# A sequential attention and feed-forward step at batch one: fewer TensorE instructions in the tail, one early touch of its program instead of two, a straight program on the sync engine

## The chip, the cores and the metric

The kernel runs on one core of one Trainium2 chip. The core has five engines with their own instruction streams: TensorE (PE, matrix products), VectorE (DVE), ScalarE (ACT), GpSimd (POOL) and SyncE (SP, here the issuer of nearly all transfers), and sixteen DMA engines that move data between HBM and the on-chip memory SBUF. Results of TensorE go to a second memory, PSUM, in eight banks. Engines wait for each other through semaphores. The metric is the device time of one execution in microseconds; smaller is better.

## What is computed

One token passes a grouped-query attention block with a cache of 65,536 positions and then a gated feed-forward block without a nonlinearity; both have a layer normalisation ahead of them and a residual addition behind.

```python
B, Sq, D = 1, 1, 512
Hq, Hkv, Sk, Dh = 32, 8, 65536, 128

def _A_ref(x, k_cache, v_cache, wq, wo):
    q = (x @ wq).reshape(B, Sq, Hq, Dh).transpose(0, 2, 1, 3)
    k = jnp.repeat(k_cache, rep, axis=1)
    v = jnp.repeat(v_cache, rep, axis=1)
    scores = jnp.einsum("bhqd,bhkd->bhqk", q, k) * (Dh ** -0.5)
    p = _softmax(scores, axis=-1)
    o = jnp.einsum("bhqk,bhkd->bhqd", p, v)
    return o.transpose(0, 2, 1, 3).reshape(B, Sq, Hq * Dh) @ wo

def _B_ref(x, w_gate, w_up, w_down):          # F = 1792
    return ((x @ w_gate) * (x @ w_up)) @ w_down

h  = x + _A_ref(_layernorm(x), k_cache, v_cache, wq, wo)
h2 = h + _B_ref(_layernorm(h), w_gate, w_up, w_down)
```

All of it is in 32-bit floats. The K and V caches alone are 537 MB, and every byte of them is read once.

## The kernel before

**Data.** The host lays K and V out as 64 chunks of 128 partitions by 16,384 floats (8.39 MB): for each of the 8 KV heads four chunks of K and then four of V. Two SBUF buffers, `kv[0]` and `kv[1]`, take the even and the odd chunks. Weights come through `wqo_sb` (the query weights of the next head beside the output weights of the present one), and at the end, when the caches are through, through the same two buffers: the gate and up weights `wg_t`, `wu_t` lie in `kv[0]`, the down weights `wd_t` in `kv[1]`, as 14 column blocks of 512 floats (numbered 0 to 13; `NC` is 14).

**The sync engine (lines 118 to 158, 479).** It issues the transfers in order. After the query weights of head 0 it jumps to a block of its program that lies far behind (`sp_far`, the lines ahead of `pe_main`) and back to `sp_main`; then come the first two chunks, and from there one chunk for each buffer that VectorE reports as free (semaphore `free`). An odd chunk raises four semaphores `s_vp`, one by the transfer and three by the sync engine's own increments, because the very last V chunk comes in four pieces (`V_CUTS`) that TensorE takes one at a time. At the end it issues the gate weights in one transfer, the up weights in three (`U_CUTS`), the down weights in six (`D_CUTS`: blocks 0-3, 4-7, 8-9, 10-11, 12, 13), and jumps to `fin`, where it waits for the result and stores four rows of `y`.

**TensorE (from `pe_main`).** It starts with two far jumps, to `pe_early` (within the first K chunk's code) and `pe_late` (between the gate and the up projection), each with one semaphore increment, and comes back to `pe_main`. In each head (`head()`): the query row for the head's four query heads (L371), turned into columns of `sm[0]` by products with a one (L375); four K chunks and four V chunks, each 32 products of 32 stationary columns (`st`) with 512 columns of the chunk (`chunk()`, L365), where four neighbouring products use four column groups of the array. Ahead of the V chunks come the softmax's maximum and the transposes of the exponentials (L380 to L387). Behind the last V chunk: the four groups of `orow` are added over partitions (L396), the softmax sums spread over all partitions (L400), and the heads' output multiplied with the output weights (L404). A product of 32-bit floats is executed as two matmul instructions, each with its own weight load; a transpose is one.

**VectorE (`dve_main` to `dve_tail`).** It sets up the constants and the first normalisation, evacuates PSUM, takes maxima, and scales. Behind the last V chunk of a head it frees the buffer, adds `orow` (L277), takes the reciprocal of the sums (L283), writes `o_pad` (L284), and adds the attention output to `acc`, the running residual (L287), where the row sum `rsum` comes along.

**The tail.** Once through the heads, the residual row `acc` must become columns. TensorE multiplies slices of `acc` with a selector (L413) and subtracts the mean in the same PSUM group (L415, `nmean`); VectorE copies it into `hn_pad` (L307). Then: the gate projection (L426, `wg_t`), the variance (L437), the up projection (L426 again, `wu_t`), the product of both with the normalisation's scale in two halves (`f_sb`, L320), its columns (L441 to L448, `f_pad`), and the down projection. Blocks below `SIDE` (8) go as one 512-wide product each, with four column groups, into `ps[1]` (L458), and VectorE adds `acc` to the four groups to give `res` (L328). The other blocks, 8 to 13, go as four 128-wide products each into `pva` (L473), and the groups of `res` are summed into the same place by products with a selector (L467). VectorE copies `pva` to `y` (L330), and the sync engine stores it (L479).

**Order.** Every engine works its own list in order. `take(e, s, n)` waits until a semaphore holds n and takes n off; `turn()` lets TensorE wait for the next step of VectorE's counter `dt` in the tail; `mine()` is VectorE's wait for its own last result.

Of the kernel before, what the change touches and what calls it, by code (L numbers as in the profile page):

```python
# [8 lines left out]
P = 128  # L9
# [34 lines left out]
def body(nc, xr, kvd, wq0, wqo, wo7, wg, wu, wd, out):  # L44
    pe_e, dve_e, act_e, pool_e, sp = nc.tensor, nc.vector, nc.scalar, nc.gpsimd, nc.sync

    def tile(name, *shape, align=32):
        return nc.alloc_sbuf_tensor(name, list(shape), F32, align_bytes=align).ap()
# [17 lines left out]
    wq_sb, wo_sb = wqo_sb[:, 0], wqo_sb[:, 1]  # L66
    xn, ln_q2 = tile("xn", P, KT), tile("ln_q2", P, KT)
    ln_s, ln_m, ln_v, ln_t, ln_r = (tile(n, 1, 1) for n in ("ln_s", "ln_m", "ln_v", "ln_t", "ln_r"))
# [40 lines left out]
    def take(e, s, n=1):  # L109
        e.wait_ge(s, n).then_inc(s, -n)  # L110
# [15 lines left out]
    sp.dma_start(wq_sb, wq0).then_inc(s_wq, 16)  # L126
    sp.br("sp_far")
    nc.switch_bb("sp_main", parent=None)
    even(0)
# [25 lines left out]
    for p, (lo, hi) in enumerate(zip(D_CUTS, D_CUTS[1:])):  # L155
        cs = slice(lo * D, hi * D)
        sp.dma_start(wd_t[:, cs], wd[:, cs]).then_inc(s_wd[p], 16)
    sp.br("fin")
    for e in (pool_e, act_e, dve_e, pe_e):
        e.br("others")  # L160
    nc.switch_bb("others", parent=None)
    dve_e.br("dve_far")
    pe_e.br("pe_early")

    take(act_e, da)
    act_e.activation(ln_t, ln_v, AF.Sqrt, bias=eps_t[0:1, 0:1], scale=1.0 / D).then_inc(ad, 1)
    pool.tick(pool_e.memset(ident, 0.0))
    pool_e.wait_ge(pool.sem, pool.n)
    c_ident = pool.tick(pool_e.affine_select(
        out=ident, in_=ident, compare_op=ALU.not_equal, fill=1.0, base=0,  # L170
        pattern=[[-1, P]], channel_multiplier=1))
    c_zero = pool.tick(pool_e.memset(qx, 0.0))
    for t in (o_pad, hn_pad, f_pad, sel_pad, acc):
        c_pads = pool.tick(pool_e.memset(t, 0.0))

    pool_e.br("fin")

    act_e.br("dve_main")
# [38 lines left out]
    with nc.Fori(0, HKV, engines=DVE_ACT):  # L217
# [41 lines left out]
        for n in range(NT):  # L259
            if n == 2:  # L260
                dve_e.sem_inc(tok, 2)
                take(dve_e, pd, 2)
                dve_e.sem_inc(da, 1)
            take(dve_e, pd)
            dve_e.tensor_copy(  # L265
                st[:, :, 0:16].rearrange("p g (b h) -> p b g h", h=REP),
                ptp[n % 2].rearrange("p (b g h) -> p b g h", b=4, h=REP)).then_inc(qt, 1)
            if n == NT - 1:
                mine(dve_e.tensor_reduce(out=l1, in_=sums, axis=AX.X, op=ALU.add))
                mine(dve_e.tensor_scalar(  # L270
                    out=l4, in0=sel_h, scalar1=l1[:, 0:1], scalar2=None, op0=ALU.mult))
# [11 lines left out]
        mine(dve_e.reciprocal(linv, sm[1][:, 0:REP]))  # L283
        dve_e.tensor_tensor(  # L284
            out=o_pad[:, :, 0], in0=sm[0][:, 0:REP], in1=linv, op=ALU.mult).then_inc(tok, 1)
        take(dve_e, pd)
        mine(dve_e.scalar_tensor_tensor(  # L287
            out=acc, in0=attn, scalar=1.0, in1=acc, op0=ALU.mult, op1=ALU.add,
            accum_out=rsum[:, 0:1]))

    take(act_e, pa)
# [3 lines left out]
    def mine(inst):  # L295
        inst.then_inc(own, 1)
        take(dve_e, own)
    dve_e.br("dve_tail")
    with nc.body("dve_far", parent=None, valid_engines=DVE_ONLY):
        dve_e.sem_inc(spare, 1)  # L300
        dve_e.br("dve_main")
    nc.switch_bb("dve_tail")
    dve_e.sem_inc(dt, 1)
# [4 lines left out]
    dve_e.sem_inc(dt, 1)  # L308
    mine(dve_e.tensor_tensor(out=ln_q2, in0=hn_pad[:, :, 0], in1=hn_pad[:, :, 0], op=ALU.mult))
# [17 lines left out]
    take(dve_e, pd)  # L327
    dve_e.tensor_tensor(out=res, in0=ps[1], in1=acc, op=ALU.add).then_inc(dt, 1)  # L328
    take(dve_e, pd)
    c_y = dve.tick(dve_e.tensor_copy(y, pva[:, 0:P]))  # L330
    dve_e.br("fin")

    with nc.body("sp_far", parent=None, valid_engines=SP_ONLY):
        sp.sem_inc(spare, 1)
        sp.br("sp_main")
    mm = pe_e.matmul
# [15 lines left out]
    def chunk(buf):  # L352
        pieces = [(0, 32, s_kv)] if not buf else [
            (lo, hi, p) for lo, hi, p in zip(V_CUTS, V_CUTS[1:], s_vp)]
        for lo, hi, p in pieces:
            take(pe_e, p, 16)
            for w in range(lo, hi):
                r, j = divmod(w, 4)
                if (buf, w) == (0, 29):
                    pe_e.br("pe_rest")  # L360
                    with nc.body("pe_early", parent=None, valid_engines=PE_ONLY):
                        pe_e.sem_inc(spare, 1)
                        pe_e.br("pe_late")
                    nc.switch_bb("pe_rest")
                i = mm(ps[buf][32 * j:32 * j + 32, :], st[:, 8 * j + r, :],  # L365
                       kv[buf][:, w * 512:(w + 1) * 512], start=(r == 0), stop=(r == 7))
        i.then_inc(kd, 1)

    def head():
        for k in range(KT):  # L370
            i = mm(ptp[0][0:1, :], xn[:, k:k + 1], wq_sb[:, k, :], start=(k == 0), stop=(k == KT - 1))  # L371
        i.then_inc(pd, 1)
        take(pe_e, tok)
        for r in range(REP):
            i = mm(sm[0][:, r:r + 1], qrow[0:1, r * P:(r + 1) * P], ones[0:1, 0:1], start=True, stop=True)  # L375
        i.then_inc(pd, 1)
        with nc.Fori(0, 4, engines=PE_ONLY) as u:
# [15 lines left out]
            chunk(1)  # L393
        take(pe_e, tok)
        for b in range(4):
            i = mm(sm[0][:, 0:REP], orow[:, b * P:(b + 1) * P], sel_b[:, 4 * b:4 * b + 4],  # L396
                   start=(b == 0), stop=(b == 3))
        i.then_inc(pd, 1)
        take(pe_e, tok)
        mm(sm[1][:, 0:REP], ones, l4, start=True, stop=True).then_inc(pd, 1)  # L400
        take(pe_e, s_w, 16)
# [6 lines left out]
    with nc.Fori(0, HKV, engines=PE_ONLY):  # L408
        head()

    turn()
    for k in range(KT):
        mm(sm[1][:, k:k + 1], acc[:, k * P:(k + 1) * P], sel_1, start=(k == 0), stop=False)  # L413
    turn()
    mm(sm[1][:, 0:KT], nmean, ones[:, 0:KT], start=False, stop=True).then_inc(pd, 1)  # L415
    turn()

    def project(acc, w, sems, c):
# [9 lines left out]
        i.then_inc(c, 1)  # L428

    project(ptp[0], wg_t, [s_wg], pa)  # L430
    pe_e.br("pe_up")
    with nc.body("pe_late", parent=None, valid_engines=PE_ONLY):
        pe_e.sem_inc(spare, 1)
        pe_e.br("pe_main")
    nc.switch_bb("pe_up")
    turn()
# [13 lines left out]
    i2.then_inc(pd, 1)  # L450
    turn()
    for c in range(SIDE):
        if c == 8:
# [6 lines left out]
    i.then_inc(pd, 1)  # L460
    if SIDE <= 8:
        turn()
    for c in range(SIDE, NC):
        if c == 12:
            turn()
            for j in range(4):
                mm(pva[32 * j:32 * j + 32, 0:P], sel_pad, res[:, j * P:(j + 1) * P],  # L467
                   start=False, stop=False)
        if c in D_CUTS:
            pe_e.wait_ge(s_wd[D_CUTS.index(c)], 16)  # L470
        for j in range(4):
            o = c * D + j * P
            i = mm(pva[32 * j:32 * j + 32, 0:P], f_pad[:, c, :], wd_t[:, o:o + P],  # L473
                   start=(c == SIDE), stop=(c == NC - 1))
    i.then_inc(pd, 1)
    pe_e.br("fin")
    nc.switch_bb("fin", parent=None)
    sp.wait_ge(dve.sem, c_y)
    sp.dma_start(out, y[0:P:32, :]).then_inc(s_out, 16)  # L479
    sp.wait_ge(s_out, 16)  # L480
# [45 lines left out]
```

## Time and profile before

| | us |
|---|---|
| median of 3 runs | 1310.52 |
| lowest, highest | 1309.73, 1310.64 |
| the profiled execution | 1310.55 |
| its span, first to last instruction | 1309.2 |
| mean granted TensorE clock | 0.745 |
| TensorE matmuls busy | 699.6 (53%) |
| VectorE busy | 108.5 (8%) |
| ScalarE busy | 55.5 (4%) |
| HBM read | 564.66 MB, 431 GB/s over the span |

The profile is of one execution. In its rows the first two numbers of an order of time are the start and the duration in us; then come the engine, the source line, the operation, the output tile and its inputs, the shape, and how many instructions were merged (xN). In brackets stands the idle time ahead of it and what ended it. PEld is TensorE's loading of stationary operands, which runs beside its matmuls. A row of a DMA issue gives the destination and the source, the size in KB (left out where it isn't known) and the median time from issue to landing. The granted clock is 1.0 when TensorE was allowed its full speed.

### The profile page before, as it was taken

The numbers are of one execution on the slowest core, as the hardware profiler recorded it, in microseconds if no ns is written. First come the engines' busy times: TensorE is split into PE (matmuls) and PEld (weight loads), VectorE is DVE, ScalarE is ACT, GpSimd is POOL, SyncE is SP. The second block draws the span as 40 slices with busy tenths as digits, with TensorE's granted clock in tenths as the row PEclk, the third lists the DMA queues.
The fourth block names the chain that finished last, engine by engine and source line by source line (L and its number), as shares of the span: only waits on it lengthen the run. The fifth ranks groups of instructions, "written<-read, shape, count | busy, mean of one in ns | idle before, by whom it ended". The sixth has DMA issues, their size and how long they took to land. (4 is left out here: it accounts for less than half of the span.)

```text
span 1309.2 us, 11334 instructions
## 1 busy us (share of the span) xinstructions
PE 699.6 (53%) x4710; PEld 225.5 (17%) x4710; DVE 108.5 (8%) x246; ACT 55.5 (4%) x107; POOL 2.8 (0%) x12
## 2 busy tenths in 40 slices
PE   4456374553754545554554636635565445545457
PEld 1112121111211111111121211111121111111113
DVE  1000010100101001000010100001010010100101
ACT  0000000000000000000000000000000000000000
POOL 0000000000000000000000000000000000000000
PEclk7676777776867768767778767868687677877687
DMA  9999999999999999999999999999999999999998
GB/s 414 422 443 437 430 445 422 443 422 445 420 445 426 441 443 424 443 422 445 420 445 424 443 439 428 443 422 443 422 445 420 445 421 446 445 422 443 422 424 361
DMA packets 12398, 564.71 MB, mean 431 GB/s; under 512 B 1382, under 2 KB 1386, under 8 KB 2155
## 3 DMA queue, kind: packets, MB, share of 16 engines
q1 hardware_dynamic: 12392, 564.67, 99.6%
q8 instruction: 2, 0.03, 0.0%
q14 instruction: 2, 0.01, 0.0%
q10 hardware_dynamic: 2, 0.00, 0.0%
HBM read 564.66 MB, written 0.00 MB: 431 GB/s over the span
## 5 line engine op out<-in xcount | busy, mean ns | idle before, releaser
L365 PE MATMUL ps<-kv,st 128*32 128x512 f32 x4096 | 579.9, 729 | 516.8 <-PEq L110 516.8
L365 PEld LDWEIGHTS ps<-kv,st 128*32 128x32 f32 x4096 | 162.0, 131 | 918.5 <-issue 918.5
L246 DVE TENSOR_REDUCE mx<-sc 128x1 f32<-128x512 f32 x32 | 21.9, 686 | 526.4 <-DVEq L110 526.4
L277 DVE TENSOR_TENSOR orow<-ps,orow 128x512 f32<-128x512 f32 x24 | 16.6, 692 | 426.9 <-DVEq L110 426.9
L387 PE MATMUL ptp<-ident,ex 128*128 128x128 f32 x128 | 27.5, 377 | 21.3 <-PEq L110 21.0
L220 ACT COPY sc<-ps 128x512 f32<-128x512 f32 x32 | 18.8, 586 | 430.8 <-ACTq L110 430.7
L224 ACT ACTIVATE ex<-sc,nbias 128x512 f32<-128x512 f32 x32 | 22.8, 714 | 305.0 <-ACTq L110 305.0
L371 PE MATMUL ptp<-wqo_sb,xn 128*1 128x512 f32 x64 | 34.0, 680 | 0.4 <-DVE xn L214 0.4
L220 ACT ACT_TABLE_LOAD x8 | 10.3, 1283 | 456.0 <-ACTq L110 456.0
L265 DVE COPY st<-ptp 128x512 f32<-128x512 f32 x32 | 22.1, 692 | 46.9 <-DVEq L110 46.9
L387 PEld LDWEIGHTS ptp<-ident,ex 128*128 128x128 f32 x128 | 21.1, 195 | 23.5 <-issue 23.5
L380 PE MATMUL sm<-ident,m 128*1 128x128 f32 x16 | 4.5, 281 | 28.1 <-PEq L110 28.1
L404 PE MATMUL attn<-wqo_sb,o_pad 128*32 128x512 f32 x64 | 12.0, 829 | 6.3 <-PEq L110 6.3
L396 PE MATMUL sm<-sel_b,orow 128*128 128x4 f32 x64 | 9.0, 264 | 8.8 <-PEq L110 8.8
L275 DVE COPY orow<-ps 128x512 f32<-128x512 f32 x8 | 5.5, 692 | 98.5 <-DVEq L110 98.5
L375 PE MATMUL sm<-ones,qrow 1*128 1x1 f32 x64 | 8.1, 244 | 7.8 <-PEq L110 7.8
L396 PEld LDWEIGHTS sm<-sel_b,orow 128*128 128x128 f32 x64 | 8.6, 208 | 16.5 <-issue 16.5
L371 PEld LDWEIGHTS ptp<-wqo_sb,xn 128*1 128x1 f32 x64 | 6.0, 95 | 28.2 <-issue 28.2
L382 PE MATMUL sm<-ones,mexp 1*128 1x1 f32 x32 | 6.6, 274 | 7.5 <-PEq L110 7.5
L375 PEld LDWEIGHTS sm<-ones,qrow 1*128 1x128 f32 x64 | 7.7, 186 | 15.1 <-issue 15.1
L380 PEld LDWEIGHTS sm<-ident,m 128*1 128x1 f32 x16 | 1.3, 79 | 42.1 <-issue 42.1
L228 DVE COPY qrow<-ptp 1x512 f32<-1x512 f32 x8 | 5.4, 678 | 27.6 <-DVEq L110 27.6
(87 smaller groups left out, 92.9 us busy)
## 6 DMA issues: line engine op xcount, KB each, us to landing
wqo_sb<-in_wqo SPq DMA_DIRECT2D x7, 2048.0 KB, 32.5
kv<-in_kv SPq DMA_DIRECT2D x1, 4096.0 KB, 22.0
kv<-in_wg SPq DMA_DIRECT2D x1, 3584.0 KB, 19.1
kv<-in_kv SPq DMA_DIRECT2D x1, 2048.0 KB, 26.5
kv<-in_kv SPq DMA_DIRECT2D x2, 1024.0 KB, 29.5
kv<-in_wd SPq DMA_DIRECT2D x2, 1024.0 KB, 18.4
kv<-in_wu SPq DMA_DIRECT2D x1, 1792.0 KB, 23.0
kv<-in_wu SPq DMA_DIRECT2D x2, 896.0 KB, 25.6
```

The lines of the kernel that those rows point to most:

```text
L220: act_e.copy(sc[s], ps[s % 2]).then_inc(ad, 1)
L224: act_e.activation(ex[s - n], sc[s], AF.Exp, bias=nbias[:, 0:1], scale=SCALE, accum_out=sums[:, s:s + 1]).then_inc(atok, 1)
L246: dve_e.tensor_reduce(out=mx[:, s:s + 1], in_=sc[s], axis=AX.X, op=ALU.max).then_inc(own, 1)
L265: dve_e.tensor_copy(st[:, :, 0:16].rearrange("p g (b h) -> p b g h", h=REP), ptp[n % 2].rearrange("p (b g h) -> p b g h", b=4, h=REP)).the ...
L277: i = dve_e.tensor_tensor(out=orow, in0=ps[n % 2], in1=orow, op=ALU.add)
L365: i = mm(ps[buf][32 * j:32 * j + 32, :], st[:, 8 * j + r, :], kv[buf][:, w * 512:(w + 1) * 512], start=(r == 0), stop=(r == 7))
L371: i = mm(ptp[0][0:1, :], xn[:, k:k + 1], wq_sb[:, k, :], start=(k == 0), stop=(k == KT - 1))
L375: i = mm(sm[0][:, r:r + 1], qrow[0:1, r * P:(r + 1) * P], ones[0:1, 0:1], start=True, stop=True)
L382: mm(sm[0][:, 0:1], mexp.rearrange("p g h -> p (g h)"), ones[0:1, 0:1], start=True, stop=True).then_inc(pd, 1)
L387: i = pe_e.transpose(ptp[half][:, b * P:(b + 1) * P], ex[half][:, b * P:(b + 1) * P], ident)
L396: i = mm(sm[0][:, 0:REP], orow[:, b * P:(b + 1) * P], sel_b[:, 4 * b:4 * b + 4], start=(b == 0), stop=(b == 3))
L404: i = mm(attn[32 * r:32 * r + 32, :], o_pad[:, r, :], wo_sb[:, r, :], start=True, stop=True)
```

## The change

1. **Sync engine:** no far jump behind its first issue. Its program is straight up to the end, where it waits for VectorE's last but one mark (`LATE`) before it goes to `fin`. The three increments per odd chunk are gone: GpSimd gives them once, for all 31 odd chunks ahead of the last, at the start.
2. **TensorE's program:** one far touch at the start (`pe_far`, in the code of the odd chunks) in place of two; a branch hint, placed ahead of the gate projection, for the jump to a block `pe_last` that holds the last column block's products and lies ahead of the code of the down projection.
3. **Columns by transposes:** for `xn` (L347), for the query rows (L375), and for `acc` in the tail (L413), where VectorE now adds up the four groups (`acol`) and then adds the mean's part.
4. **Order in a head:** the softmax sums' product stands ahead of the four `orow` products; the last V buffer of a head is freed after the `orow` addition; TensorE starts a head only when `acc` is written.
5. **Down projection:** `SIDE` is 12: blocks 8 to 11 join the 512-wide group, and arrive in one transfer (`D_CUTS`); `res` is written in two halves; block 12 and the selector products come ahead of block 13, which waits for its own transfer.
6. **Store:** all 128 rows of `y` are stored, and the host picks the four.

```diff
-SIDE = 8
+SIDE = 12
+LATE = 2
-D_CUTS = (0, 4, 8, 10, 12, 13, 14)
+D_CUTS = (0, 4, 8, 12, 13, 14)
...
     def odd(g):
         sp.dma_start(kv[1], kvd[g]).then_inc(s_vp[0], 16)
-        for p in s_vp[1:]:
-            sp.sem_inc(p, 16)
...
-    sp.br("sp_far")
-    nc.switch_bb("sp_main", parent=None)
+    pe_e.br("pe_far")
+    dve_e.br("dve_far")
...
+    for p in s_vp[1:]:
+        pool_e.sem_inc(p, 16 * (end // 2 - 1))
...
+    sp.wait_ge(dve.sem, LATE)
     sp.br("fin")
...
     c_ones = dve.tick(dve_e.memset(ones, 1.0))
+    dve_e.sem_inc(tok, 1)
...
             take(dve_e, kd)
-            dve_e.sem_inc(free, 1)
+            if n < NT - 1:
+                dve_e.sem_inc(free, 1)
...
-                i.then_inc(tok, 2)
-        take(dve_e, pd, 2)
+                i.then_inc(tok, 1)
+        dve_e.sem_inc(free, 1)
+        take(dve_e, pd)
         mine(dve_e.reciprocal(linv, sm[1][:, 0:REP]))
+        take(dve_e, pd)
         dve_e.tensor_tensor(
             out=o_pad[:, :, 0], in0=sm[0][:, 0:REP], in1=linv, op=ALU.mult).then_inc(tok, 1)
...
             accum_out=rsum[:, 0:1]))
+        dve_e.sem_inc(tok, 1)
...
-    mine(dve_e.tensor_copy(hn_pad[:, :, 0], sm[1][:, 0:KT]))
-    dve_e.sem_inc(dt, 1)
+    mine(dve_e.tensor_reduce(
+        out=acol, in_=ptp[1].rearrange("p (k j x) -> p k j x", k=KT, j=4)[:, :, :, 0], axis=AX.X,
+        op=ALU.add))
+    take(dve_e, pd)
+    dve_e.tensor_tensor(out=hn_pad[:, :, 0], in0=sm[1][:, 0:KT], in1=acol, op=ALU.add).then_inc(dt, 1)
+    dve_e.wait_ge(dt, 4)
...
-    dve_e.tensor_tensor(out=res, in0=ps[1], in1=acc, op=ALU.add).then_inc(dt, 1)
+    for half in range(2):
+        cs = slice(half * 256, half * 256 + 256)
+        dve_e.tensor_tensor(out=res[:, cs], in0=ps[1][:, cs], in1=acc[:, cs], op=ALU.add).then_inc(dt, 1)
+    dve.n += 1
+    assert dve.n == LATE
+    dve_e.sem_inc(dve.sem, 1)
...
-        i = mm(ps[0][:, k:k + 1], xn_row[0:1, k * P:(k + 1) * P], ones[0:1, 0:1], start=True, stop=True)
+        i = pe_e.transpose(ps[0][:, k:k + 1], xn_row[0:1, k * P:(k + 1) * P], ident[0:1, 0:1])
...
+            if (buf, lo) == (1, 16):
+                pe_e.br("pe_rest")
+                with nc.body("pe_far", parent=None, valid_engines=PE_ONLY):
+                    pe_e.sem_inc(spare, 1)
+                    pe_e.br("pe_main")
+                nc.switch_bb("pe_rest")
...
     def head():
+        take(pe_e, tok)
...
         take(pe_e, tok)
+        mm(sm[1][:, 0:REP], ones, l4, start=True, stop=True).then_inc(pd, 1)
+        take(pe_e, tok)
         for b in range(4):
             i = mm(sm[0][:, 0:REP], orow[:, b * P:(b + 1) * P], sel_b[:, 4 * b:4 * b + 4],
                    start=(b == 0), stop=(b == 3))
         i.then_inc(pd, 1)
-        take(pe_e, tok)
-        mm(sm[1][:, 0:REP], ones, l4, start=True, stop=True).then_inc(pd, 1)
...
-    turn()
+    take(pe_e, tok)
     for k in range(KT):
-        mm(sm[1][:, k:k + 1], acc[:, k * P:(k + 1) * P], sel_1, start=(k == 0), stop=False)
-    turn()
-    mm(sm[1][:, 0:KT], nmean, ones[:, 0:KT], start=False, stop=True).then_inc(pd, 1)
+        i = pe_e.transpose(ptp[1][:, k * P:(k + 1) * P], acc[:, k * P:(k + 1) * P], ident)
+    i.then_inc(pd, 1)
+    turn()
+    mm(sm[1][:, 0:KT], nmean, ones[:, 0:KT], start=True, stop=True).then_inc(pd, 1)
...
+    near = pe_e.mark_branch_hint_location()
     project(ptp[0], wg_t, [s_wg], pa)
-    pe_e.br("pe_up")
-    with nc.body("pe_late", parent=None, valid_engines=PE_ONLY):
-        pe_e.sem_inc(spare, 1)
-        pe_e.br("pe_main")
-    nc.switch_bb("pe_up")
...
+    def single(c):
+        pe_e.wait_ge(s_wd[D_CUTS.index(c)], 16)
+        for j in range(4):
+            o = c * D + j * P
+            i = mm(pva[32 * j:32 * j + 32, 0:P], f_pad[:, c, :], wd_t[:, o:o + P],
+                   start=(c == SIDE), stop=(c == NC - 1))
+        return i
+
+    pe_e.br("pe_down")
+    with nc.body("pe_last", parent=None, valid_engines=PE_ONLY):
+        single(NC - 1).then_inc(pd, 1)
+        pe_e.br("fin")
+    nc.switch_bb("pe_down")
...
-    if SIDE <= 8:
-        turn()
-    for c in range(SIDE, NC):
...
+    for c in range(SIDE, NC - 1):
+        single(c)
+    for j in range(4):
+        if j % 2 == 0:
             turn()
...
+        mm(pva[32 * j:32 * j + 32, 0:P], sel_pad, res[:, j * P:(j + 1) * P], start=False, stop=False)
+    pe_e.br("pe_last").branch_hint(near)
...
-    sp.dma_start(out, y[0:P:32, :]).then_inc(s_out, 16)
+    sp.dma_start(out, y).then_inc(s_out, 16)
```

More of the change, by code (lines that the diff above doesn't have):

```diff
@@ L66, in body @@
     wq_sb, wo_sb = wqo_sb[:, 0], wqo_sb[:, 1]
-    xn, ln_q2 = tile("xn", P, KT), tile("ln_q2", P, KT)
+    xn, ln_q2, acol = (tile(n, P, KT) for n in ("xn", "ln_q2", "acol"))
     ln_s, ln_m, ln_v, ln_t, ln_r = (tile(n, 1, 1) for n in ("ln_s", "ln_m", "ln_v", "ln_t", "ln_r"))
@@ L122, in odd @@
         sp.dma_start(kv[1], kvd[g]).then_inc(s_vp[0], 16)
-        for p in s_vp[1:]:
-            sp.sem_inc(p, 16)
     sp.dma_start(wq_sb, wq0).then_inc(s_wq, 16)
-    sp.br("sp_far")
-    nc.switch_bb("sp_main", parent=None)
+    pe_e.br("pe_far")
+    dve_e.br("dve_far")
+    take(act_e, da)
+    act_e.activation(ln_t, ln_v, AF.Sqrt, bias=eps_t[0:1, 0:1], scale=1.0 / D).then_inc(ad, 1)
+    act_e.br("dve_main")
+    pool.tick(pool_e.memset(ident, 0.0))
+    pool_e.wait_ge(pool.sem, pool.n)
+    c_ident = pool.tick(pool_e.affine_select(
+        out=ident, in_=ident, compare_op=ALU.not_equal, fill=1.0, base=0,
+        pattern=[[-1, P]], channel_multiplier=1))
+    c_zero = pool.tick(pool_e.memset(qx, 0.0))
+    for p in s_vp[1:]:
+        pool_e.sem_inc(p, 16 * (end // 2 - 1))
+    for t in (o_pad, hn_pad, f_pad, sel_pad, acc):
+        c_pads = pool.tick(pool_e.memset(t, 0.0))
+    pool_e.br("fin")
     even(0)
@@ L157, in body @@
         sp.dma_start(wd_t[:, cs], wd[:, cs]).then_inc(s_wd[p], 16)
+    sp.wait_ge(dve.sem, LATE)
     sp.br("fin")
[L159 to L178, printed above, removed]
     nc.switch_bb("dve_main", parent=None)
     c_ones = dve.tick(dve_e.memset(ones, 1.0))
+    dve_e.sem_inc(tok, 1)
     dve_e.memset(mean_m, 1.0 / D).then_inc(own, 1)
@@ L331, in body @@
     dve_e.br("fin")
-    with nc.body("sp_far", parent=None, valid_engines=SP_ONLY):
-        sp.sem_inc(spare, 1)
-        sp.br("sp_main")
+    with nc.body("dve_far", parent=None, valid_engines=DVE_ONLY):
+        dve_e.sem_inc(spare, 1)
+        dve_e.br("dve_main")
     mm = pe_e.matmul
@@ L374, in head @@
         for r in range(REP):
-            i = mm(sm[0][:, r:r + 1], qrow[0:1, r * P:(r + 1) * P], ones[0:1, 0:1], start=True, stop=True)
+            i = pe_e.transpose(sm[0][:, r:r + 1], qrow[0:1, r * P:(r + 1) * P], ident[0:1, 0:1])
         i.then_inc(pd, 1)
@@ L409, in body @@
         head()
+    take(pe_e, tok)
+    for k in range(KT):
+        i = pe_e.transpose(ptp[1][:, k * P:(k + 1) * P], acc[:, k * P:(k + 1) * P], ident)
+    i.then_inc(pd, 1)
     turn()
-    for k in range(KT):
-        mm(sm[1][:, k:k + 1], acc[:, k * P:(k + 1) * P], sel_1, start=(k == 0), stop=False)
-    turn()
-    mm(sm[1][:, 0:KT], nmean, ones[:, 0:KT], start=False, stop=True).then_inc(pd, 1)
+    mm(sm[1][:, 0:KT], nmean, ones[:, 0:KT], start=True, stop=True).then_inc(pd, 1)
     turn()
```

32 lines of the change are left out of this document (4 added, 28 removed).

## The prediction

> **What bounds the kernel now.** I read the summary of the profile first, its share of busy DMA engines ahead of the compute engines' shares.
>
> ```profile
> span 1309.2 us, 11334 instructions
> ...
> DMA  9999999999999999999999999999999999999998
> ...
> q1 hardware_dynamic: 12392, 564.67, 99.6%
> ```
>
> The sixteen DMA engines are occupied in every one of the 40 slices. So the kernel is one stream of 564.67 MB from start to end, and a change can only count where the stream could run dry, where it starts, or behind its last byte. The second view is the list of DMA issues, for the time from issue to landing (last column, us), over all chunks and for the single issue at 357.86 us, and after it the order of time on the sync queue.
>
> ```profile
> kv<-in_kv SPq DMA_DIRECT2D x63, 29.0
> ...
> kv<-in_kv SPq DMA_DIRECT2D x1, 25.9
> ...
> wqo_sb<-in_wq SPq DMA_DIRECT2D x1, 1024.0 KB, 6.1
> ...
> 0.75 0.40 SPq L126 DMA_DIRECT2D wqo_sb<-in_wq  x1
> 1.61 0.33 SPq L119 DMA_DIRECT2D kv<-in_kv  x1
> ```
>
> A chunk is 8.39 MB (128 rows of 16384 floats), which at 564.67 MB in about 1304 us takes 19.4 us. Its median landing is 29.0 us after the issue, so it is queued some 9.6 us ahead of need; at 357.86 us, where I found the shortest lead, 25.9 - 19.4 = 6.5 us. At the start the second transfer is issued at 1.61 us, while the first, issued at 0.75, lands 6.1 us later, at 6.85: 5.2 us of cover. The third view is the windows at the end (columns: stretch, its length, PE, PEld, DVE, ACT, POOL busy, granted TensorE clock, DMA share, GB/s), with the landings of the pieces of `wd` issued 1282.56, 1283.51 and 1284.45 us after the start.
>
> ```profile
> 1303.00:1304.00 1.00, 1.00 (x13) 0.48 (x16) 0.34 (x2) 0.00 (x0) 0.00 (x0) 1.00 1.02 397
> 1304.00:1305.00 1.00, 1.00 (x16) 0.29 (x12) 0.00 (x0) 0.00 (x0) 0.00 (x0) 1.00 0.22 84
> ...
> 1282.56 0.43 SPq L157 DMA_DIRECT2D kv<-in_wd  x1
> kv<-in_wd SPq DMA_DIRECT2D x1, 1024.0 KB, 19.4
> kv<-in_wd SPq DMA_DIRECT2D x1, 512.0 KB, 21.0
> 1284.45 2.24 SPq L157 DMA_DIRECT2D kv<-in_wd  x1
> kv<-in_wd SPq DMA_DIRECT2D x1, 256.0 KB, 21.3
> ```
>
> Column blocks 4-7 of `wd` land at 1282.56 + 19.4 = 1302.0, block 11 at 1283.51 + 21.0 = 1304.5, block 13 at 1284.45 + 21.3 = 1305.75. The stream ends there; 3.45 us of the span lie behind it. Last, the order of time from the last V piece to the end, the chain that runs beside those landings.
>
> ```profile
> 1277.76 1.06 PE L365 MATMUL ps<-kv,st 128*32 128x512 f32 x8 [0.59 <-PEq L110]
> 1280.20 1.74 PE L365 MATMUL ps<-kv,st 128*32 128x512 f32 x8 [1.37 <-PEq L110]
> 1283.02 1.84 PE L396 MATMUL sm<-sel_b,orow 128*128 128x4 f32 x8 [1.09 <-PEq L110]
> 1284.72 0.57 PE L400 MATMUL sm<-l,ones 128*128 128x4 f32 x2
> 1285.44 0.18 DVE L283 RECIPROCAL linv<-sm 128x4 f32<-128x4 f32 x1 [2.56 <-DVEq L110]
> 1285.77 0.17 DVE L284 TENSOR_TENSOR o_pad<-sm,linv 128x4 f32<-128x4 f32 x1
> 1288.19 0.69 DVE L287 SCALAR_TENSOR_TENSOR acc<-attn,acc 128x512 f32<-128x512 f32 x1 [2.25 <-DVEq L110]
> 1289.44 1.87 PE L413 MATMUL sm<-sel,acc 128*128 128x1 f32 x8 [1.42 <-DVEq L303]
> 1291.17 0.57 PE L415 MATMUL sm<-ones,nmean 128*128 128x4 f32 x2
> 1292.26 5.80 PE L426 MATMUL ptp<-kv,hn_pad 128*32 128x448 f32 x32 [0.52 <-DVEq L308]
> 1298.30 3.21 PE L426 MATMUL ps<-kv,hn_pad 128*32 128x448 f32 x32
> 1301.70 0.81 DVE L320 SCALAR_TENSOR_TENSOR f_sb<-ps,ln_r,g_sb 128x256 f32<-128x256 f32 x2 [2.71 <-DVEq L110]
> 1303.22 1.92 PE L458 MATMUL ps<-kv,f_pad 128*32 128x512 f32 x16
> 1305.33 0.69 DVE L328 TENSOR_TENSOR res<-ps,acc 128x512 f32<-128x512 f32 x1 [1.71 <-DVEq L110]
> 1306.08 0.42 PE L467 MATMUL pva<-res,sel_pad 128*32 128x128 f32 x8
> 1306.32 0.62 PE L473 MATMUL pva<-kv,f_pad 128*32 128x128 f32 x16
> 1307.12 0.29 DVE L330 COPY y<-pva 128x128 f32<-128x128 f32 x1 [1.10 <-DVEq L110]
> 1307.43 0.67 SPq L479 DMA_DIRECT2D out_y<-y  x1
> ```
>
> TensorE's last matmul ends at 1306.94, 1.2 us after the last landing, because the down projection could begin only at 1303.22. Chain and stream end almost together: from 1305.75 the last two blocks (16 matmuls in 0.62) could have been done at 1306.37, so the chain is late by about 0.6 us.
>
> **The change, part by part.** *Start.* The sync engine loses one jump between its first two issues (0.46 us idle at 1.15 to 1.61) and 16-step semaphore increments per odd chunk. Behind 5.2 us of cover that gives 0; without the cover it would be 0.46 at most. Transposes for the columns of `xn` and `q` halve their matmuls, a gain under the leads above: 0. *Every head.* TensorE now waits at a head's beginning for `acc` (one 0.69 us DVE operation and two hand-offs, about 1.1 us); the next head's query matmuls, the qrow copy and `st` are queued behind it, and K chunk 0 behind those. The last V buffer of a head is freed after the `orow` addition, 0.7 us later. Together 1.8 us per head against a shortest lead of 6.5: 0; with the lead gone it would be 8 x 1.8 = 14 us.
>
> *Tail up to the gate.* The matmul for the softmax sums (L400, 0.57) moves ahead of L396 and under the `orow` addition, and the reciprocal with it: the reciprocal began 0.15 behind the end of L400 (1285.29), and `o_pad` will begin that far behind the end of L396 (1284.86), at 1285.0 instead of 1285.77: -0.8. The signal for `acc` is given inside the loop, ahead of the loop's end and the old jump to the tail: 1288.88 to 1289.44 was 0.56, an ordinary hand-off is 0.2: -0.3. L413's 1.87 becomes four transposes; their price is at most that of the row below for eight, halved.
>
> ```profile
> 1251.03 1.33 PE L387 MATMUL ptp<-ident,ex 128*128 128x128 f32 x8 [1.23 <-PEq L110]
> ...
> 1269.38 0.33 SPq L150 DMA_DIRECT2D kv<-in_wg  x1
> kv<-in_wg SPq DMA_DIRECT2D x1, 3584.0 KB, 19.1
> ```
>
> 0.67 instead of 1.87: -1.2. A new reduce over 16 columns, priced like the 0.17 of `o_pad`, lies beside L415. So the gate projection starts about 2.3 us earlier, near 1289.95 (`wg` has landed by then, at 1269.38 + 19.1 = 1288.5).
>
> *What is late next.* These 2.3 us do not reach the end. With the gate and the up projection costing what they did, the down projection could start near 1300.9, but its blocks 4-7 land at 1302.0 and 8-11 at 1304.5. From there the chain is the stream's. `SIDE` 12 puts blocks 8-11 into the group that passes through `res`, and one transfer instead of two carries them, so all of this group ends behind the landing of block 11. Step by step: 1304.5, 0.1 until TensorE has it, 1.06 for eight matmuls (the row at 1277.76) = 1305.67; 0.19 to DVE (1305.14 to 1305.33 before); two halves of `res` at 0.41 and 0.40 (the two `f_sb` halves took 0.81) = 1306.67; 0.06 hand-off; two of four `res` groups, the jump and block 13. For the jump no row stands alone: 0 below, 0.41 above (0.56 less an ordinary DVE hand-off of 0.15, which held a loop end and a jump); I take 0.2, the middle. Four plus eight matmuls go by the 16 in 0.62: 0.5. That makes 1307.43 for TensorE, against 1306.94: **+0.49**. Block 12 lands between 1304.5 and 1305.75 and is done under `res`: 0.
>
> *Output.* The whole `y` is 64 KB in place of 2 KB. A full 128-row issue takes 0.33 to 0.43, the four-row one took 0.67: -0.3. The bytes cost 0 at the least, 0.43 (another issue) at the most; I take 64 KB at the stream's rate of 0.43 MB per us, +0.15. Sum -0.1 to -0.15, between -0.34 and +0.19; I take -0.1. The sync engine's wait and late jump lie under the last matmuls: 0, or 0.2 if they don't.
>
> **Sum:** +0.49 - 0.1 = +0.4. The profiled execution took 1310.55 us, 1.35 more than its span; so 1310.55 + 0.4 = 1310.95, rounded to **1310.9** (the median of before, 1310.52, is the same run for run).
>
> *The clock.* One term hangs on the granted clock: eight such matmuls cost 1.06 at 1277.76 and 1.74 at 1280.20.
>
> ```profile
> 1275.00:1280.00 5.00, 2.99 (x25) 0.68 (x24) 0.00 (x0) 0.00 (x0) 0.00 (x0) 1.00 1.06 453
> 1280.00:1285.00 5.00, 3.72 (x18) 2.19 (x18) 0.69 (x1) 0.00 (x0) 0.00 (x0) 0.55 1.05 453
> ```
>
> The clock fell at 1280 after waits for V pieces of no more than 1.4 us. Waits of that size come into the new tail ahead of block 8. [...] I therefore keep half clock as a case.
>
> **Rivals.** *Half clock in the last 3 us:* +0.68 for blocks 8-11 (1.74 - 1.06) and, by the same ratio 1.64, +0.32 for the last twelve: 1310.9 + 1.0 = 1311.9. For it: waits ahead of 1302.0 and 1304.5. Against: the gate and up projection are dense before.
>
> *The tail gains after all:* if the jump is free, and the halves of `res` overlap TensorE better, and the output gains 0.35, then 1310.9 - 0.2 - 0.3 - 0.25 = 1310.15. No more: behind 1305.75 lie the last block, `y` and 1.77 of output (1307.43 to the span's end at 1309.2).
>
> *Slower than before, an instruction fetch in the tail:* before, TensorE touched two far places of its program at the start; now only one, and it jumps back to `pe_last` just ahead of the last block.
>
> ```profile
> q8 instruction: 1, 0.02, 8.0%
> ...
> q8 instruction: 1, 0.02, 0.6%
> ```
>
> They are from the windows 2 to 3 and 10 to 20 us: two fetches of 16 KB, and the DMA view from 20 us to the end lists none. The first took 8.0% of sixteen engines in 1 us, 1.28 us. With a round trip no longer than the output's 1.77, a jump to code that isn't there costs 1.3 to 3.05 us; I take the upper end, since it had to queue behind `wd`: 1310.9 + 3.05 = 1313.95. It decides only if it falls behind 1304.5; earlier the waits for `wd` swallow it. For it: the early touch of the third stretch of code is gone. Against: the hint is placed ahead of the gate projection, 5.80 us of cover, and `pe_last` stands just ahead of code that TensorE has run. [...]
>
> *The change does nothing:* chain and stream trade places, 1310.5; this is inside my range.
>
> **How the numbers follow.** Forecast 0.46 (own range 1310.3 to 1311.5); half clock 0.22; tail gains or nothing, 1310.15 to 1310.5, 0.13; fetch in the tail 0.14; more than 0.2% faster 0.05, which would need a faster stream, since even a span that ended with the last landing and the bare output would be 1305.75 + 1.77 + 1.35 = 1308.9. The range 1309.6 to 1314.0 holds all but the rim of the last two. Within 0.2% (2.6 us, about what a measurement of this kernel can tell from no change) lie the first three cases and the nearer end of the fetch; slower, beyond 1313.1, is most of the fetch case and a little of what I don't see: 0.15. Within: 0.80.
>
> **What would show it.** The last `wd` landing still near 1305.75; L404 and the gate 0.8 and 2.3 us earlier; the down projection waiting for blocks 4-7 and 8-11; `res` starting near 1305.9 and `y` near 1307.6. An instruction fetch near 1290 with no idle behind it speaks against the rival, TensorE idle ahead of `pe_last` for it. I am wrong if the stream's end moves, or DMA shows a gap between heads.

## The result, and the profile after

| | before | after |
|---|---|---|
| median, lowest, highest of 22 runs each, us | 1310.05, 1309.54, 1310.98 | 1311.91, 1310.94, 1313.11 |
| ratio after to before, 95% interval | | 1.0014 [1.0008, 1.0021] |
| the profiled execution, us | 1310.55 | 1312.96 |
| its span, us | 1309.2 | 1311.7 |

The changed kernel is 1.86 us slower, 0.14%. That is inside the predicted range and within the 0.2%, but 1.0 us above the predicted 1310.9. Its profiled run is one of its slower ones.

The summary of the changed kernel's profile answers to the rows shown of before:

```profile
span 1311.7 us, 11131 instructions
...
DMA  9999999999999999999999999999999999999997
...
q1 hardware_dynamic: 12384, 564.73, 99.5%
```

There are 203 fewer instructions, the stream is as dense as before, and only its last slice is thinner: the loss lies behind the stream. The order of time of the tail shows where:

```profile
1281.59 0.39 PE L400 MATMUL sm<-l,ones 128*128 128x4 f32 x2
1284.15 1.06 PE L409 MATMUL attn<-wqo_sb,o_pad 128*32 128x512 f32 x8 [0.46 <-PEq L111]
1286.38 1.09 PE L418 MATMUL ptp<-ident,acc 128*128 128x128 f32 x4 [1.17 <-PEq L111]
1288.95 4.78 PE L432 MATMUL ptp<-kv,hn_pad 128*32 128x448 f32 x32 [1.26 <-DMA kv<-in_wg]
1297.54 0.96 PE L432 MATMUL ps<-kv,hn_pad 128*32 128x448 f32 x8 [1.09 <-DMA kv<-in_wu]
1300.44 1.07 PE L473 MATMUL ps<-kv,f_pad 128*32 128x512 f32 x8 [0.18 <-issue]
1302.41 1.94 PE L473 MATMUL ps<-kv,f_pad 128*32 128x512 f32 x8 [0.90 <-DMA kv<-in_wd]
1305.00 1.93 PE L473 MATMUL ps<-kv,f_pad 128*32 128x512 f32 x8 [0.65 <-DMA kv<-in_wd]
1306.67 0.68 PE L458 MATMUL pva<-kv,f_pad 128*32 128x128 f32 x8
1307.10 0.75 DVE L329 TENSOR_TENSOR res<-ps,acc 128x256 f32<-128x256 f32 x2 [6.50 <-DVEq L111]
1308.16 0.82 PE L458 MATMUL pva<-kv,f_pad 128*32 128x128 f32 x8
1309.13 0.29 DVE L334 COPY y<-pva 128x128 f32<-128x128 f32 x1 [1.28 <-DVEq L111]
1309.45 0.34 SPq L485 DMA_DIRECT2D out_y<-y  x1
```

What the reader is to see: the chain up to the gate is 3.3 us earlier (1288.95 against 1292.26) and then has nothing to do but wait. The gate starts when `wg` lands, the last part of the up projection when `wu` lands, blocks 4 and 8 when `wd` lands; each of these rows names a DMA as what ended its idle time. Blocks 0 to 3 took 1.07, blocks 4 to 7 and 8 to 11 took 1.94 and 1.93 at half clock. The windows over the same stretch (second figure the length, ahead of the DMA share the granted clock):

```profile
1299.00:1302.41 3.41, 2.11 (x18) 1.10 (x18) 0.83 (x4) 0.00 (x0) 0.00 (x0) 1.00 1.00 423
1302.41:1305.80 3.39, 2.74 (x12) 0.43 (x16) 0.00 (x0) 0.00 (x0) 0.00 (x0) 0.50 0.47 181
1305.80:1309.20 3.40, 2.95 (x32) 1.19 (x24) 0.82 (x3) 0.00 (x0) 0.00 (x0) 0.50 0.00 0
```

The clock fell behind a stretch in which TensorE's matmuls were busy for 2.11 of 3.41 us, with no wait longer than 0.90. And the output, in the DMA view of 1309 to 1311 us:

```profile
q1 hardware_dynamic: 144, 0.07, 12.3%
q8 instruction: 1, 0.02, 4.1%
issues: line engine op xcount, KB each, median us to landing
out_y<-y SPq DMA_DIRECT2D x1, 64.0 KB, 2.1
```

The store lands 2.1 us after its issue, and beside it runs a 16 KB instruction fetch (4.1% of sixteen engines in 2 us, 1.3 us). From issue to the span's end it is about 2.2 us, against about 1.8 before (a span is given to 0.1 us). The last piece of `wd` landed at 1306.1 here, at 1305.8 in the version with four rows below, and at 1305.75 before: the stream's end didn't move by more than it differs from run to run.

Every run has a span of its own. Over the 22 runs of the changed kernel the spans lie between 1309.7 and 1311.8, median 1310.55. In four later sets of runs of the kernel before (33, 27, 21, 21) the medians are 1308.5, 1308.5, 1308.3 and 1308.4, so the profiled span of 1309.2, on which the prediction built its sum, was 0.7 to 0.9 long.

### The profile page after: what moved, and what is told of

The parts are those of the page before. It is cut to its first block, busy times and chain, and to the rows that moved or that the text cites. A ratio compares the mean times of both kernels' runs of the same rounds, so it can differ in the third digit from the quotient of the medians.

```text
span 1311.7 us, 11131 instructions
## 1 busy us (share of the span) xinstructions
PE 695.5 (53%) x4646; PEld 216.3 (16%) x4646; DVE 108.5 (8%) x248; ACT 55.4 (4%) x107; POOL 2.8 (0%) x12
## 5 line engine op out<-in xcount | busy, mean ns | idle before, releaser
L369 PE MATMUL ps<-kv,st 128*32 128x512 f32 x4096 | 571.9, 721 | 515.2 <-PEq L111 515.2
L376 PE MATMUL ptp<-wqo_sb,xn 128*1 128x512 f32 x64 | 42.1, 821 | 9.8 <-PEq L111 9.8
L380 PE MATMUL sm<-ident,qrow 1*128 1x1 f32 x32 | 3.0, 194 | 7.8 <-PEq L111 7.8
L387 PEld LDWEIGHTS sm<-ones,mexp 1*128 1x128 f32 x32 | 5.3, 206 | 10.3 <-issue 9.1
```

Source lines behind the costliest of these rows:

```text
L387: mm(sm[0][:, 0:1], mexp.rearrange("p g h -> p (g h)"), ones[0:1, 0:1], start=True, stop=True).then_inc(pd, 1)
```

## The experiments

"TensorE's end" below is the start of the last row of its products plus its duration. Times are medians; a ratio is to the kernel before, with its 95% interval.

**Store of four rows.** The changed kernel with

```diff
-    sp.dma_start(out, y).then_inc(s_out, 16)
+    sp.dma_start(out, y[0:P:32, :]).then_inc(s_out, 16)
```

> The changed kernel with the old store of four rows, nothing else. Theory (the store of all 128 rows spreads over sixteen DMA engines, and one of them is still busy with a 16 KB instruction fetch that TensorE's last jump sets off at 1309.21): from the issue of the store to the span's end 1.75 us as before, in place of 2.25, and the time 0.5 us below the changed kernel's 1311.9, 1311.4. Rival (the store costs nothing, the difference is jitter): 1311.9 and still about 2.2 us from issue to end.

1311.63, ratio 1.0011 [1.0002, 1.0020]. Its profiled run had a full clock to the end:

```profile
1304.67 1.07 PE L473 MATMUL ps<-kv,f_pad 128*32 128x512 f32 x8 [1.52 <-DMA kv<-in_wd]
1305.91 0.76 DVE L329 TENSOR_TENSOR res<-ps,acc 128x256 f32<-128x256 f32 x2 [5.63 <-DVEq L111]
1306.97 0.43 PE L458 MATMUL pva<-kv,f_pad 128*32 128x128 f32 x8
1307.89 0.65 SPq L485 DMA_DIRECT2D out_y<-y  x1
```

From the issue to the span's end (1309.7) it is about 1.8 us, as before. The median fell by 0.28, less than the 0.5 expected, and the two intervals overlap: by the times the gain is not separated from nothing. The rows are the forecast's own steps: `res` at 1305.91 (forecast 1305.86) and TensorE's end at 1307.40 (forecast 1307.43).

**Old down projection.** The changed kernel with its core taken back:

```diff
-SIDE = 12
+SIDE = 8
-D_CUTS = (0, 4, 8, 12, 13, 14)
+D_CUTS = (0, 4, 8, 10, 12, 13, 14)
...
-    for half in range(2):
-        cs = slice(half * 256, half * 256 + 256)
-        dve_e.tensor_tensor(out=res[:, cs], in0=ps[1][:, cs], in1=acc[:, cs], op=ALU.add).then_inc(dt, 1)
+    dve_e.tensor_tensor(out=res, in0=ps[1], in1=acc, op=ALU.add).then_inc(dt, 1)
```

and with blocks 8 to 11, then the `res` products, then 12 and 13 on TensorE.

> The changed kernel with the old down projection (512-wide blocks 0 to 7, narrow blocks 8 to 13, res in one piece, ahead of block 12). Theory (the group that passes through res now waits for the landing of block 11, and the whole tail behind it runs at half clock): res is done before 1304.5 and only narrow blocks stand behind the last landing, so TensorE ends near 1306.6 in place of 1308.98, and the time falls by 1.5 to 2.4 us, to 1309.5 to 1310.4. Rival (the jump to pe_last and its fetch cost the time): TensorE still ends 2 us or more behind the last landing, time above 1311.

1310.38, ratio 1.0002 [0.9993, 1.0011]: 1.53 less than the changed kernel, at the upper rim of what was expected.

```profile
1302.16 1.93 PE L472 MATMUL ps<-kv,f_pad 128*32 128x512 f32 x8 [0.53 <-DMA kv<-in_wd]
1304.28 0.69 DVE L327 TENSOR_TENSOR res<-ps,acc 128x512 f32<-128x512 f32 x1 [3.94 <-DVEq L111]
1305.93 0.43 PE L457 MATMUL pva<-kv,f_pad 128*32 128x128 f32 x8 [0.17 <-DMA kv<-in_wd]
1306.85 0.34 SPq L485 DMA_DIRECT2D out_y<-y  x1
```

Blocks 4 to 7 ran at half clock here too (1.93), and it cost nothing: `res` was ready by 1305.0 all the same, and only block 13 stood behind its landing. The jump to `pe_last` and the full store with a fetch beside it are still in this version, so they are not the bulk of the loss.

**Extra products ahead of blocks 4 and 8.** The changed kernel with

```diff
+        if c in (4, 8):
+            for d in range(c // 2 + 2):
+                j = d % 4
+                mm(ptp[0][32 * j:32 * j + 32, :], f_pad[:, j, :], wd_t[:, j * D:(j + 1) * D],
+                   start=True, stop=True)
```

> The changed kernel with 4 and 6 extra products of blocks already there, into an unused PSUM bank, while TensorE waits for blocks 4 and 8; they keep it busy and change no result. Theory (half clock): the granted clock stays at 1.00 from 1300 to 1309 in most runs, blocks 8 to 11 take 1.06 us in place of 1.93, and the time falls by 1.0 to 1.4 us, to 1310.5 to 1310.9, with a smaller spread between runs. Rival (the clock falls anyway, or the order of the tail alone is the cost): clock near 0.5 at the end, or no gain: 1311.6 or more.

1312.38, ratio 1.0015 [1.0006, 1.0024]: a miss. In its profiled run the clock had fallen at 1300.57, ahead of the first extra product, and was full again from 1303.98:

```profile
1300.57:1303.98 3.41, 3.41 (x20) 0.87 (x16) 0.00 (x0) 0.00 (x0) 0.00 (x0) 0.50 0.96 393
1303.98:1307.00 3.02, 3.02 (x32) 0.92 (x26) 0.00 (x0) 0.00 (x0) 0.00 (x0) 1.00 0.05 17
```

So the first four extra products ran at half clock (eight matmuls in 1.95), and the six that start at 1304.44 held back blocks 8 to 11, which had landed at 1304.56, to 1307.2. It tells that the clock can fall before the waits for `wd`, and that these products cost more than they could save; about the worth of a full clock it tells nothing.

**No jump.** The changed kernel without `pe_last`, its jump and the hint; block 13 stands in line.

```diff
-    near = pe_e.mark_branch_hint_location()
...
-    pe_e.br("pe_last").branch_hint(near)
+    single(NC - 1).then_inc(pd, 1)
+    pe_e.br("fin")
```

> The changed kernel without the block pe_last, its jump and the hint: block 13's products stand at the program's end. Theory of the clock and the landings: the time stays within 0.4 us of 1311.9; the instruction fetch at the end may vanish, which would take up to 0.5 us from the store. Rival (the fetch or jump is what costs): TensorE shows an idle stretch of 1.3 us or more ahead of a fetch in the tail, or the time falls by more than 1 us.

1311.81, ratio 1.0012 [1.0003, 1.0021]; 0.10 from the changed kernel, not separated. The instruction fetch moved: the window 1292 to 1293 us lists one, the window 1309 to 1310 none, and the store of 64 KB landed 0.6 us sooner. That gain of the profiled run doesn't show in the median.

```profile
q8 instruction: 1, 0.02, 6.0%
...
1308.27 0.34 SPq L480 DMA_DIRECT2D out_y<-y  x1
...
out_y<-y SPq DMA_DIRECT2D x1, 64.0 KB, 1.5
```

**The kernel before with the new down projection alone** (the first diff of the old one turned round, block 13 last, without the jump).

> The kernel before with the new down projection alone (512-wide blocks 0 to 11, one transfer for 8 to 11, res in two halves, block 13 last, without the jump). Theory (the new order puts res and its products behind blocks 8 to 11): those blocks end near 1306.0 in place of 1305.1 for blocks 0 to 7, and TensorE ends 0.5 us later at full clock, 1.0 to 1.8 later where the clock falls, so the time is 1310.6 to 1311.8. Rival (the new order costs only together with the earlier chain): 1310.0 to 1310.3.

1311.33, ratio 1.0009 [1.0000, 1.0018], 1.22 above the 1310.11 of the kernel before, measured beside it. The interval begins at 1, but the spans hardly overlap: 1309.3 to 1310.2, median 1309.75, against 1308.2 to 1309.3, median 1308.5. The profiled run had full clock, blocks 8 to 11 at 1305.29 for 1.06 and TensorE's end at 1307.96. So the new order costs without the earlier chain too.

```profile
1305.29 1.06 PE L460 MATMUL ps<-kv,f_pad 128*32 128x512 f32 x8 [1.53 <-DMA kv<-in_wd]
1307.48 0.48 PE L474 MATMUL pva<-kv,f_pad 128*32 128x128 f32 x6
```

**Combined:** the changed kernel with the old down projection, four rows and no jump.

> The changed kernel with the old down projection, the old store of four rows and no jump to pe_last: what is left of the change is the straight sync engine, the transposes, the earlier chain and the one early touch. Theory (the stream's last landing is then the bound and only block 13 stands behind it): TensorE ends near 1306.3, 0.6 us before the kernel before, and the time is 1309.3 to 1309.7, 0.4 to 0.7 below the kernel before. Rival (the last landing comes later or the gain goes into the output): 1310.0 or more.

1309.91, ratio 0.9998 [0.9989, 1.0007]. TensorE ended where expected, at 1306.34, but the median is short of the 1309.7 expected and only 0.2 below the 1310.11 of before: not separated from it, 2.0 below the changed kernel. By their spans (medians 1308.6 and 1308.5) nothing is gained on the kernel before.

```profile
1304.16 0.69 DVE L327 TENSOR_TENSOR res<-ps,acc 128x512 f32<-128x512 f32 x1 [3.74 <-DVEq L111]
1305.37 0.97 PE L456 MATMUL pva<-kv,f_pad 128*32 128x128 f32 x16
1306.84 0.65 SPq L480 DMA_DIRECT2D out_y<-y  x1
```

**The kernel before with the full store alone**, one run:

> The kernel before with the store of all 128 rows alone. Theory (the store is slow only when a 16 KB instruction fetch runs beside it): no fetch stands at the end here, and from issue to the span's end it takes 1.5 to 1.75 us. Rival (sixteen engines or 64 KB are slower in themselves): 2.0 us or more.

1311.24, with a span of 1309.9. There was a fetch beside the store after all, in the window 1307 to 1309, and the store was the slowest of all runs:

```profile
q8 instruction: 1, 0.02, 4.5%
...
1306.76 0.34 SPq L479 DMA_DIRECT2D out_y<-y  x1
...
out_y<-y SPq DMA_DIRECT2D x1, 64.0 KB, 3.1
```

The premise (no fetch here) was wrong; a slow store and a fetch stood together again. In the trace fifteen of the sixteen parts of this store landed by 1308.30 and the last at 1309.82; in the changed kernel fifteen by 1311.00 and the last at 1311.57. Over the five profiles with a full store and a fetch beside it the last part comes 0.57 to 1.52 us behind the fifteenth; in the one without a fetch (no jump) 0.04. Why the kernel before shows no fetch at its end in its own profile, and this one does, is open. The run has a second use: it is another profile of the old tail, with `f_sb` at 1299.51 in place of 1301.70.

```profile
1290.56 5.30 PE L426 MATMUL ptp<-kv,hn_pad 128*32 128x448 f32 x32 [0.52 <-DVEq L308]
1303.31 0.69 DVE L328 TENSOR_TENSOR res<-ps,acc 128x512 f32<-128x512 f32 x1 [1.89 <-DVEq L110]
1305.29 0.96 PE L473 MATMUL pva<-kv,f_pad 128*32 128x128 f32 x16
```

**Combined, without the early touch.**

> The combined version (e6) without the one early touch of TensorE's program. Theory (the early 16 KB fetch runs while the first packets are slow, puts one DMA engine 1.4 to 2.1 us behind the other fifteen, and this lag stays in the queue to the last landing): without it the slowest engine is at most 1.0 us behind, the last landing of wd is near 1305.0 in place of 1305.8, and the time falls by 0.5 us or more below e6; TensorE's own wait for the code in head 0 hides under the lead of the chunks. Rival (the fetch comes anyway, and the lag with it): last landing at 1305.6 to 1305.9 and the time of e6.

1310.02, ratio 0.9997 [0.9988, 1.0006]. The first transfer landed 5.5 us after its issue in place of 6.5 with the touch, and the trace lists no fetch at the start (the first stands at 34 us); but the last piece of `wd` landed at 1305.96 (1305.88 with the touch). The theory that the early fetch sets the last landing fell. Most of this run's tail was at half clock (0.50 from 1299.24 to 1306.06), and TensorE still ended at 1306.79: with the old order half clock cost 0.45 us (1306.34 in the combined version). In every trace the last of the sixteen DMA engines lands its part of a `wd` piece 1.4 to 2.2 us after the first; what makes it trail stays open.

**Extra products in four gaps**, a second try at the clock. The changed kernel with 4, 2, 4 and 5 products ahead of the last piece of `wu`, the `f_sb` columns, and blocks 4 and 8:

```diff
+    def spin(n, st_, w):
+        for d in range(n):
+            j = d % 4
+            mm(attn[32 * j:32 * j + 32, :], st_, w[:, j * 512:(j + 1) * 512], start=True, stop=True)
```

> The changed kernel with 4, 2, 4 and 5 extra products into an unused PSUM bank in the four gaps of its tail: ahead of the last piece of the up weights, ahead of the f_sb columns, ahead of blocks 4 and 8; they change no result. In e3 the clock had fallen already from a window that began at 1297, ahead of its extra products. Theory (the half clock of the tail is what lies between the 1310.9 of the sum and the measured 1311.9): with all gaps filled the clock stays at 1.00 to the end, blocks 8 to 11 take 1.06 us, res starts near 1306.0, TensorE ends near 1307.4 to 1307.6, and the median is 1310.9 to 1311.5, 0.4 to 1.0 under the changed kernel. Rival (the clock isn't the cause, or extra products cost what they save): 1311.8 or more, or the clock falls again.

1312.05, ratio 1.0015 [1.0006, 1.0024]: no gain. In the first try the granted clock was 1.00 from 1297.20 to 1300.57, and 0.50 only from there. The clock held in the profiled run (blocks 4 to 7 took 1.06, blocks 8 to 11 1.12), and TensorE ended at 1307.38; the spans drew together (1310.0 to 1311.1, median 1310.4). But the part of the time outside the span was 1.55 to 1.83 us in all eleven runs, where the changed kernel has 1.24 to 1.49.

**The kernel before with the straight sync engine and one touch alone:**

> The kernel before with the straight sync engine and one far touch of TensorE's program alone; chain, down projection and store as before. Theory (the start is covered by 5.2 us of queued transfer, and no fetch stalls TensorE): 1310.1, within 0.4 us of the kernel before, last landing of wd between 1305.7 and 1306.4. Rival (the one touch leaves a fetch in the tail that stalls TensorE, or the earlier second issue moves the stream): the time differs by 1 us or more, or TensorE stands idle for 1 us ahead of code in the tail without a landing or another engine to wait for.

1310.08 against 1310.05, ratio 0.9999 [0.9990, 1.0008], last landing at 1306.02. The start is free, as predicted. It is a third profile of the old tail:

```profile
1305.52 0.97 PE L463 MATMUL pva<-kv,f_pad 128*32 128x128 f32 x16
```

**The new down projection against the combined version, without and with the extra products.**

> The changed kernel with the old store of four rows and without the jump to pe_last: against e6 it differs in the new down projection alone. Theory (behind the landing of block 11 the new order has 1.06 us of products, two halves of res, the selector products and block 13 in series, at full clock 0.9 to 1.1 us more than the old order, and more where the clock halves): the span's median is 1309.8 to 1310.3 and the time 1311.1 to 1311.6, 1.2 to 1.7 above e6. Rival (the cost of the new order came with the store and the jump): within 0.5 us of e6's 1309.9.

> The same as e11 with the extra products of e9 in the four gaps, so that it differs from e11 in the clock of the tail alone (they change no result). Theory (the clock makes the spread and about 0.3 us of the median): spans lie within 0.7 us of each other, near 1309.5 to 1309.8, against a spread of more than 1.2 us in e11, and their median is 0.2 to 0.6 below. Rival (the clock is nearly all of the cost): the span falls to e6's 1308.6 to 1308.9. Other rival (the clock has no part): spread and median of e11.

The first: 1311.62, ratio 1.0012 [1.0003, 1.0021], spans 1309.5 to 1311.3, median 1310.3; 1.71 above the combined version, which has all else in common. The two were not measured side by side: each against the kernel before beside it, they are 1.82 slower and 0.20 faster, 2.0 apart. The second: 1311.94, ratio 1.0013 [1.0004, 1.0022], median span 1310.0: five spans of 1309.6 or 1309.7, six of 1310.0 to 1310.9. So the extra products didn't hold the spread together in all runs, and how much of the median the clock makes stays open. The two profiled runs show what it makes of one run, the first at half clock, the second at full:

```profile
1304.69 1.93 PE L467 MATMUL ps<-kv,f_pad 128*32 128x512 f32 x8 [0.66 <-DMA kv<-in_wd]
1307.92 0.50 PE L457 MATMUL pva<-kv,f_pad 128*32 128x128 f32 x6
```

```profile
1304.68 1.11 PE L477 MATMUL ps<-kv,f_pad 128*32 128x512 f32 x8
1306.95 0.48 PE L465 MATMUL pva<-kv,f_pad 128*32 128x128 f32 x6
```

Blocks 8 to 11 start at the same time, and TensorE ends at 1308.42 and 1307.43: 1.0 us for the clock. Full clock alone doesn't bring back the combined version's 1306.34: the other 1.1 us is the order.

## Why the prediction was right, and where its sizes were off

The forecast was right that the kernel gets slower by less than 0.2%, and that the place is the down projection behind the landing of blocks 8 to 11. Its size was not right: the sum said +0.4, the medians say +1.86.

- **Start and heads, 0.** Right: the straight sync engine with one touch alone is 0.03 us from before, and DMA shows no gap between heads.
- **The earlier chain, 2.3 us that don't reach the end.** Right in kind. The 3.3 us by which the gate starts earlier are counted from a late run: in the three other profiles of the old chain the gate starts at 1290.28 to 1290.67, 1.3 to 1.7 behind the changed kernel's. The waits for blocks 4 and 8 of `wd` were named; those for `wg`, which was to have landed before the gate, and for the last part of `wu` were not. With the old down projection behind it, without the jump and with four rows, the chain is worth 0.2 us, not separated from nothing.
- **The new down projection, +0.49.** The steps to TensorE's end at 1307.43 were right to 0.03 us where the clock was full (1307.40 and 1307.43). In part that is luck: from the end of `res` to TensorE's end it takes 0.73 with the jump (four rows) and 0.68 without (the last of the runs above), so the jump cost nearer 0.05 than 0.2, and the twelve matmuls more than 0.5. The term was too small because of the end that it was measured from: 1306.94 came from a run of the kernel before whose gate ran at half clock for most of its 5.80 us (granted 0.50 until 1297.52), and whose chain was late. In the two other profiles of the old tail the chain is earlier, waits for the landings, and TensorE ends at 1305.29 + 0.96 = 1306.25 and at 1306.49. Against these and the combined version's 1306.34 the new order costs about 1.1 us at full clock (1307.43) and 2.1 at half (1308.42). By medians the term is 1.2 (alone in the kernel before), 1.5 (taken out of the changed kernel) and 1.7 (alone against the combined version; 2.0 when each is taken against the kernel before measured beside it) in place of 0.49.
- **Half clock, a rival at 1311.9.** It happened in the profiled run (0.50 from 1302.41 to 1309.2), and one run at half clock is 1.0 us longer than one at full, as the rival had it. It isn't needed for the whole of the loss: 1.1 us stand at full clock. That the rival's 1311.9 is also the measured median is luck: it starts 0.5 too high and holds a down projection 0.7 or more too cheap. How much the clock makes of the median, the two tries with extra products don't show. Here, as at 1280 in the kernel before, the clock fell behind short waits: between 1299.00 and 1302.41 none was longer than 0.90 us, in the kernel before none longer than 1.37 between 1275 and 1280.2.
- **The output, -0.1.** Wrong in sign in the profiled runs: about 2.2 us against 1.8. By the medians the cost is not separated from nothing: 0.28 with and without the full store, 0.47 between the old down projection and the combined version (store and jump together), and only 0.10 without the jump, where the store landed 0.6 us sooner. The issue got shorter (0.34 against 0.67), as predicted; what the sum left out is a last part of the store that comes late where an instruction fetch runs beside it (0.57 to 1.52 us behind the fifteenth, 0.04 without a fetch).
- **The fetch in the tail as a stall of TensorE, 1313.95.** Didn't happen: the products of block 13 follow at once (1308.16, with no idle time ahead of them). The fetch came at 1309.21, behind the last products (1308.98) and beside the store. No run here shows TensorE stalled at the jump, and without the jump the time is 0.10 us away. The 1.3 to 3.05 us of a stall were the prediction's estimate, from a fetch at the start (1.28 us) and the output (1.77); no run shows such a stall.
- **The level.** The sum began at 1310.55, 0.5 above the median of 22 runs. It hid part of the missing cost, so that the 1.0 us between forecast and result looks smaller than the error of the sum, 1.5.

## What to carry to other kernels

When a stream of transfers sets the end, count only what stands in series behind each of its last landings: putting more work into the group that passes through another engine and back moved that trip from behind an early landing to behind a late one (the waits for them ended at 1302.41 and 1305.00 in the changed kernel). Look at several spans of the old kernel before a sum of tenths of a microsecond is built on one of them. The 3.3 us won ahead of the gate turned into waits here (1.26 for `wg`, 1.09 for the last part of `wu`, 0.90 and 0.65 for `wd`). In three of the four profiles that have the earlier chain, the new down projection and no extra products, the clock fell to 0.50 between 1301 and 1303 (blocks 4 to 7 took 1.92 to 1.94 us, 1.06 in the fourth); in both with all four gaps filled it held (1.06).

## What was not expected

- A small store over all sixteen DMA engines landed 1.5 us after its issue with no instruction fetch beside it (one profile), and 2.1 to 3.1 us with one (five profiles). What the fetch does to the store is read from this pairing alone. With four rows a fetch beside the store did no harm: about 1.8 us from issue to the span's end with it and without.
- The time holds a part outside the span that isn't constant: 1.24 to 1.49 us in all 22 runs of the changed kernel, but 1.25 to 2.73 in the kernel before, over 1.5 in 46 of its 102 runs, and 1.57 to 1.66 in all ten runs of the kernel before with the new down projection. It takes back some of the 2.1 us by which the spans differ. No view of the profile shows what happens there.
